# Second layer's tiles as 4, 4, 4, 4 and 1 instead of 4, 4, 4, 3 and 2, with quarter-sum products in the fourth block too

## The chip, the cores and the metric

The kernel runs on one core of one Trainium2 chip. The metric is the device time of one execution in microseconds (us); lower is better. Before the change the median of 3 runs is 708.11 us (707.74 to 708.77).

## What is computed

Cross attention between 512 tokens and 32 states for 4 batches of 8 heads, then two dense layers over the 4 x 544 = 2176 rows that come out of it (17 tiles of 128 rows), each with an activation between its two weight matrices:

```python
attn_out = _attn_ref(x, state)                 # (4, 8, 544, 64)
x = attn_out.transpose(0, 2, 1, 3).reshape(2176, 512)
h = x @ w_in                                   # 512 -> 2048
x = elu(h) @ w_out                             # 2048 -> 512, first layer
h = x @ w2_in                                  # 512 -> 2048, second layer
g = h * np.tanh(np.log1p(np.exp(np.minimum(h, 20.0))))
out = g @ w2_out                               # 2048 -> 512
```

The results are float32. The change is in the second layer alone.

## The kernel before, in words

**Products.** To multiply in float32 with TensorE's single-pass type float32r, an operand is split into a high half (rounded by a copy to float32r) and a low half (what is left). A product of two operands is then three instructions: high x high, high x low, low x high. They are lines 935 to 937 (first multiplication, `mm1`: 128 x 128 of `w_in` is loaded into the array, the rows of x stream through), 1138 to 1140 (second multiplication, `mm2`: 128 x 128 of the activation g is loaded, 512 columns of `w_out` stream) and 1066 to 1068 (the same with quarter sums). Where an operand is not split (line 911, the first layer's state tile; line 776, the attention's scores), a float32 product is issued as two instructions by the compiler.

**The second layer.** `BLOCKS2` (line 39) gives its blocks as (first tile, tiles): four tiles each in blocks 0, 1 and 2, three in block 3, two in block 4. A block goes through 16 steps, one for each slice j of 128 of the 2048 hidden units. A step is `mm1` (4 parts of the contraction x 3 instructions of 128 columns per tile), `hidden` (the activation on ScalarE and VectorE, lines 991 to 1002, and the split of g) and, two steps later, `mm2` (3 instructions of 512 columns for each tile of the block).

**Quarter sums.** Blocks in `SEVEN` (1 and 2) do the second multiplication by Strassen's scheme: for a pair of slices, a 2 x 2 arrangement of quarters of g and of w_out is multiplied with seven products instead of eight. `g_sums` makes the sums of g's quarters on VectorE; those of w_out (the factors) are made once, kept in device memory (`f2d`, `h2d`) and loaded again for each pair (`load_factors`). `seven_products` issues 7 x 6 instructions of 256 columns per pair, two of the seven behind the even step's `mm1` and five behind the odd step's. The seven results lie in seven of the eight PSUM banks, so each `mm1` shares the one that is left, and ScalarE copies it out at once (line 974). After a block's last pair the seven results are copied out and added up (`result_sums`, line 1087) during the next block's steps.

**The last two blocks** multiply plainly. Their steps go in groups of four (`GROUP`): four `mm1` in a row, then the four `mm2` held back. `halves_back` loads the split w_out again (16 x 512 KB) when block 2 ends. In block 4 the last results are copied in two halves by ScalarE and VectorE and stored by both queues (`retire`, lines 1173 to 1185).

**Order.** Every operation goes into `Plan` with a cost, its predecessors and a due time; `T` holds the due time of each step, summed from modelled costs (`mm(n)` = n / 2400 + 0.013 us). `Plan.run` then plays the operations and writes an order for each engine: the operation that can start first goes first, among equals the one that is due first. On the chip each engine follows its order. Buffers come from tags with a fixed number of places (`w_in` and `w_out`: 16 each; `o`: 4), and a load waits until a place is free. Loads and stores are issued by SP, in order.

Of the kernel before, what the change touches and what calls it, by code (L numbers as in the profile page):

```python
# [37 lines left out]
STATE_AT = NC  # L38
BLOCKS2 = [(0, 4), (4, 4), (8, 4), (12, 3), (15, 2)]

# [195 lines left out]
def attention_elu_mish(  # L236
# [95 lines left out]
    first2 = len(steps)  # L332
    steps += [(2, blk, t0, n, j) for blk, (t0, n) in enumerate(BLOCKS2) for j in range(NF)]
    index = {(k, b, j): s for s, (k, b, _, _, j) in enumerate(steps)}

    def mm1_cost(kind, blk, n, j):
        if kind == 0:
            return 16 * mm(4 * P)
        if kind == 1:
            return 2 * mm(4 * S) if (blk, j) in WHOLE else 6 * mm(S)  # L340
        return 12 * mm(n * P)

# [7 lines left out]
    for s, (kind, blk, t0, n, j) in enumerate(steps):  # L350
        c = mm1_cost(kind, blk, n, j) + (mm2_cost(kind, n, whole_out(kind, blk, j)) if kind < 2 else
                                         (30 if j % 2 else 12) * mm(HALF_E) if blk in SEVEN else n * 3 * mm(DM))
        T.append(T[-1] + c + (PACE_FIRST if s < NF // 2 else PACE if s < first2 else 0.0))
# [181 lines left out]
    def halves_back(j):  # L535
        w = w_sb["out", 2, j] = buf("w", "w_out", NF, [P, 2, DM], F32R, f"w_again{j}_")
        add(SP, 512.0, lambda: nc.sync.dma_start(out=w.t.bitcast(F32), in_=h2d[:, j]), r=[("h2d", j)],
            w=[(w, 0), (w, 1)], after=[products[max(products) - (j < NF // 2)][FREED[j % 8]]], lag=2.0)

# [357 lines left out]

    def apart(s):
        kind, blk, t0, n, j = steps[s]
        return kind == 2 and n < MAXC and j % GROUP < 2  # L900

    def mm1(s):
# [4 lines left out]
        if kind == 0:  # L907
            for i in range(NC):
                def f(i=i):
                    for k in range(NK):  # L910
                        nc.tensor.matmul(h[:, i * P:(i + 1) * P], lhsT=place_w1(j * NC + i, k),  # L911
                                         rhs=sread[:, k, :], start=(k == 0), stop=(k == NK - 1))

                sl = j * NC + i
                A("PE", 4 * mm(4 * P), f, w=[h], due=due,
                  r=[(w1[sl // 2], sl % 2)] + [("sread", b) for b in range(B)])
        elif kind == 1 and (blk, j) in WHOLE:
            for k in range(2):
                def f(k=k):
                    m = m_sb[blk, j // NC][:, k, j % NC * P:(j % NC + 1) * P]  # L920
                    nc.tensor.matmul(h.t, lhsT=m, rhs=x1[blk][:, k, :], start=(k == 0), stop=(k == 1))  # L921

                add("PE", mm(4 * S), f, w=[h], due=due,
                    r=[(m_sb[blk, j // NC], j % NC, q) for q in range(2)] + [(x1[blk], k)])
        else:
            nk = 2 if kind == 1 else NK
            for k in range(nk):
                def f(k=k):
                    if kind == 1:
                        wh, wl = (m_hl[s][:, i, k, :] for i in range(2))  # L930
                        xh, xl = (x1hl(blk)[:, i, k, :] for i in range(2))
                    else:
                        wh, wl = (w_sb["in", 2, j][:, i, k * P:(k + 1) * P] for i in range(2))
                        xh, xl = (x2[blk][i][:, k, :n] for i in range(2))
                    nc.tensor.matmul(h[:, :n], lhsT=wh, rhs=xh, start=(k == 0), stop=False)  # L935
                    nc.tensor.matmul(h[:, :n], lhsT=wh, rhs=xl, start=False, stop=False)  # L936
                    nc.tensor.matmul(h[:, :n], lhsT=wl, rhs=xh, start=False, stop=(k == nk - 1))  # L937

                if kind == 1:
                    r = [(m_hl[s], 0), (m_hl[s], 1), (x1hl(blk), k)]  # L940
                else:
                    w = w_sb["in", 2, j]
                    r = [(w, 0), (w, 1), (x2[blk][0], k), (x2[blk][1], k)]
                add("PE", 3 * mm(n), f, r=r, w=[h], due=due)
        return h

    def hidden(s, h):
# [4 lines left out]
        if kind < 2:  # L952
# [15 lines left out]
            split_g(g, e, 0, n, [e])  # L968
            return
        u = buf("l2", "u", 2, [P, MAXN])  # L970
        g = None
        if seven or kind == 2 and s - index[2, max(SEVEN), NF - 1] in COPIED:
            ps, h = h, buf("work", "wraw", 3, [P, MAXN], F32, "hs")
            add("ACT", act(n * P), lambda n=n: nc.scalar.copy(h[:, :n * P], ps[:, :n * P]), r=[ps], w=[h])
        if seven:
            pass
        elif apart(s):
            g = buf("l2", "g", 2, [P, 2, n * P], F32R, "g")
        else:
            g = buf("work", "g", GBUFS, [P, 2, MAXN], F32R, "g")  # L980
        gs[s] = g
        last = s == len(steps) - 1
        parts = [(0, n // 2), (n // 2, n)] if last else [(0, n)]
        if g:
# [23 lines left out]

    evens, g_factors = {}, {}

# [37 lines left out]
    def seven_products(s):  # L1048
# [8 lines left out]
        for o, k in enumerate(SEVEN_ORDER):  # L1057
# [4 lines left out]
            def run(a=acc[k], g=g[gi], gc=gc, f=f[fi], fc=fc):  # L1062
                for q in range(2):
# [6 lines left out]
            made[k] = add("PE", 6 * mm(HALF_E), run, r=gk + fk, w=[acc[k]],  # L1070
                          due=T[s + 1 + (o >= 2)] + SEVEN_DUE + 0.5 * o)
        if p < NF // 2 - 1:
            return
        due = T[s + 2] + 2.0
        o = {c: buf("work", "o", OBUFS, [P, DM], F32, f"o{blk}_{c}_") for c in ("11", "12", "21", "22")}
# [5 lines left out]
        for i, sums in enumerate(SUMS):  # L1081
            begin(s + SUMS_AT[i], result_sums, sums, v, t0)

    def result_sums(sums, v, t0):

        for to, a, b, op in sums:
            add("DVE", 0.605, lambda to=to, a=a, b=b, op=op: nc.vector.tensor_tensor(
                v[to].t, v[a].t, v[b].t, getattr(ALU, op)), r=[v[a], v[b]], w=[v[to]])
            if to in RESULTS:
                i, e = RESULTS[to]  # L1090
                for q in range(2):
                    add(SP, 128.0, lambda to=to, q=q, t=t0 + 2 * i + q, e=e: nc.sync.dma_start(
                        out=out_rows(t)[..., e * HALF_E:(e + 1) * HALF_E],
                        in_=v[to][:, q * HALF_E:(q + 1) * HALF_E]), r=[v[to]], due=T[len(steps)])

# [6 lines left out]
    def mm2(s, only=None):  # L1102
# [7 lines left out]
        if part not in accs:  # L1110
            tags = ["h"] if kind == 0 else [f"acc{i}" for i in range(NK if kind == 1 else n)]
            accs[part] = [spot(t, f"acc{kind}_{blk}_{t}_") for t in tags]
# [4 lines left out]
        due = T[s + 2]  # L1117
        made = []
        for i in (range(NC if kind < 2 else n) if only is None else only):
            acc = accs[part][0 if kind == 0 else i]  # L1120
# [28 lines left out]
    def retire(kind, blk, j, acc, s):  # L1149
        due = T[s + 2] + 4.5  # L1150

# [119 lines left out]
    for j in range(NF):  # L1271
        begin(index[1, 3, j], reload, "in", j)
        begin(min(index[1, 3, j] + 1, first2), reload, "out", j)
        begin(index[2, max(SEVEN), NF - 1] + 1 + j // 4, halves_back, j)
    for p in range(NF // 2):
        g = index[2, min(SEVEN) - 1, 0] + FACTORS_FROM + int(p * FACTORS_STEP)
        begin(g, make_factors, p, T[g + FACTORS_TO])
    for blk in sorted(SEVEN):
        for p in range(NF // 2):
            begin(index[2, blk, 0] + 2 * p if blk > min(SEVEN) or p > 1 else index[2, blk, 0] - 4 + 2 * p,  # L1280
                  load_factors, blk, p)
    for blk in range(len(BLOCKS2)):
        begin(first2 + NF * (blk - 1) + 6 if blk else s_state + NQ + 4, load_x2, blk)
    if WHOLE_J < NF:
# [4 lines left out]

    narrow = next(index[2, blk, 0] for blk, (_, n) in enumerate(BLOCKS2) if n < MAXC)  # L1290
    held = []
    for s in range(len(steps) + 2):
        if s < len(steps):
            kind, blk, t0, n, j = steps[s]
            if s == s_state + NQ + 3:

                switch.append(add("X", 0.0, flip, after=attention, due=T[first2] - 40.0))
            gate[:] = [*turn, *first] if s == narrow else turn if s > narrow else []
            h = mm1(s)
            turn = first = [plan.ops[-1]]  # L1300
            gate[:] = turn
            for f, args in later.pop(s, ()):
                f(*args)
            gate[:] = []
            hidden(s, h)
        if s < len(steps) and s >= narrow and (s - narrow) % GROUP < GROUP - 1 and \
                not (steps[s - 2][0] == 2 and steps[s - 2][1] in SEVEN):
            held.append(s - 2)
            continue
        if s == len(steps):  # L1310
            for i in range(BLOCKS2[-1][1]):
                for q in range(s - 2, s):
                    mm2(q, [i])
        elif s >= 2 and s < len(steps):
            gate[:] = turn if held else []
            turn = []
            for q in (*held, s - 2):
                turn = mm2(q)
                if held:
                    gate[:] = turn[-1:]  # L1320
                for j in after_step.pop(q, ()):
                    split_weight("out", 1, j, w_sb["whole", 1, j])
            held.clear()
            gate[:] = []
    assert not later
# [14 lines left out]
HALF_E = DM // 2  # L1340
SEVEN = {1, 2}
FIRST = [(0, 0, HALF), (1, 0, HALF), (0, HALF, NF), (1, HALF, NF), (2, 0, NF), (3, 0, NF)]
# [11 lines left out]
OBUFS = 4  # L1354
GROUP = 4
STATES_LATE = None
# [17 lines left out]
FREED = (1, 7, 4, 4, 6, 6, 3, 3)  # L1374
COPIED = (1,)
LATE_COPY = 0.0
# [32 lines left out]
```

## Time and profile before

| | |
|---|---|
| median of 3 runs | 708.11 us (707.74 to 708.77) |
| the profiled execution | 707.95 us |
| its span | 706.1 us |
| TensorE busy | 701.0 us, 99% |
| weight loads busy | 592.5 us, 84% |
| VectorE / ScalarE busy | 584.5 us (83%) / 452.9 us (64%) |

The span runs from the first to the last instruction; the execution has 1.85 us more around it. PE is TensorE's matmul, PEld its weight load (it overlaps PE), DVE VectorE, ACT ScalarE, SP the engine that issues most DMAs. Times in rows are us from the span's start unless marked ns. The time of one matmul in a row includes its way through the array; matmuls overlap, so their spacing is shorter. The chain of waits follows the work that ended last: each of its pieces begins where the one before it ends.

### The profile page before, as it was taken

The numbers are of one execution on the slowest core, as the hardware profiler recorded it, in microseconds if no ns is written. First come the engines' busy times: TensorE is split into PE (matmuls) and PEld (weight loads), VectorE is DVE, ScalarE is ACT, GpSimd is POOL, SyncE is SP. The second block draws the span as 40 slices with busy tenths as digits, with TensorE's granted clock in tenths as the row PEclk, the third lists the DMA queues.
The fourth block names the chain that finished last, engine by engine and source line by source line (L and its number), as shares of the span: only waits on it lengthen the run. The fifth ranks groups of instructions, "written<-read, shape, count | busy, mean of one in ns | idle before, by whom it ended". The sixth has DMA issues, their size and how long they took to land.

```text
span 706.1 us, 12109 instructions
## 1 busy us (share of the span) xinstructions
PE 701.0 (99%) x4370; PEld 592.5 (84%) x4370; DVE 584.5 (83%) x1176; ACT 452.9 (64%) x840; POOL 12.0 (2%) x26
## 2 busy tenths in 40 slices
PE   9999999999999999999999999999999999999998
PEld 7478787877888788888888888989989989999987
DVE  7999998969787867887889987798888998776575
ACT  4987775655666744675666657666776767554454
POOL 1000100100000000000000000000000000000000
PEclk9999999999999999999999999999999999999999
DMA  9846788374797877668778896665566459400100
GB/s 296 290 148 194 225 196 231 93 153 86 242 245 253 259 258 251 227 220 293 237 257 310 267 344 222 222 204 164 182 184 225 152 176 365 153 15 31 46 1 30
DMA packets 113826, 140.31 MB, mean 199 GB/s; under 512 B 48872, under 2 KB 77544, under 8 KB 113768
## 3 DMA queue, kind: packets, MB, share of 16 engines
q1 hardware_dynamic: 113352, 139.36, 61.9%
q8 instruction: 34, 0.56, 0.3%
q10 hardware_dynamic: 416, 0.20, 0.1%
q14 instruction: 24, 0.20, 0.1%
HBM read 101.25 MB, written 38.27 MB: 198 GB/s over the span
## 4 chain that ended last, share of the span: by engine, by line
PE 97%; DVE 1%; ACT 1%; DMA 1%; SPq 0%; issue 0%
PE acc_acc L1138 13%; PE h L935 13%; PE h L936 13%; PE h L937 13%; PE acc_acc L1140 13%; PE acc_acc L1139 13%; PE m L1068 4%; PE m L1067 4%; PE m L1066 4%; PE fold L614 2%; PE h L911 2%; PE h L921 1%; DMA st_raw<-in_state 1%; PE sr L859 1%; PE acc_acc L1126 1%; PE acc_h L1138 1%
## 5 line engine op out<-in xcount | busy, mean ns | idle before, releaser
L935 PE MATMUL h<-x,w_in 128*128 128x512 f32 (+2 forms) x320 | 114.6, 358 | 0.0
L936 PE MATMUL h<-x,w_in 128*128 128x512 f32 (+2 forms) x320 | 114.6, 358 | 0.0
L937 PE MATMUL h<-x,w_in 128*128 128x512 f32 (+2 forms) x320 | 114.2, 357 | 0.0
L1098 ACT CAST g<-e 128x512 fp32r<-128x512 f32 (+3 forms) x116 | 66.3, 572 | 68.1 <-PE acc_acc L1140 35.7
L1138 PE MATMUL acc_acc<-g,w_out 128*128 128x512 f32 x252 | 100.3, 398 | 0.0
L1139 PE MATMUL acc_acc<-g,w_out 128*128 128x512 f32 x252 | 98.2, 390 | 0.0
L1140 PE MATMUL acc_acc<-g,w_out 128*128 128x512 f32 x252 | 98.1, 389 | 0.0
L1099 DVE TENSOR_TENSOR g<-e,g 128x512 fp32r<-128x512 f32 (+3 forms) x116 | 72.9, 629 | 23.3 <-ACT g L1098 22.3
L996 ACT ACTIVATE e<-u,two 128x512 f32<-128x512 f32 (+3 forms) x81 | 53.0, 656 | 36.6 <-DVE u L994 36.5
L937 PEld LDWEIGHTS h<-x,w_in 128*128 128x128 f32 x320 | 60.3, 189 | 7.7
L935 PEld LDWEIGHTS h<-x,w_in 128*128 128x128 f32 x320 | 60.5, 189 | 7.0
L936 PEld LDWEIGHTS h<-x,w_in 128*128 128x128 f32 x320 | 60.5, 189 | 6.7
L1000 DVE TENSOR_TENSOR u<-u,e 128x512 f32<-128x512 f32 (+3 forms) x81 | 48.7, 603 | 19.7 <-ACT e L998 18.0
L1068 PE MATMUL m<-f,g 128*128 128x256 f32 x224 | 63.4, 283 | 0.0
L1067 PE MATMUL m<-f,g 128*128 128x256 f32 x224 | 63.4, 283 | 0.0
L1066 PE MATMUL m<-f,g 128*128 128x256 f32 x224 | 63.2, 282 | 0.0
L955 ACT ACTIVATE e<-h 128x512 f32<-128x512 f32 x68 | 40.3, 597 | 33.4 <-PE h L937 21.3
L1138 PEld LDWEIGHTS acc_acc<-g,w_out 128*128 128x128 f32 x252 | 47.4, 188 | 12.8 <-issue 1.7
L1140 PEld LDWEIGHTS acc_acc<-g,w_out 128*128 128x128 f32 x252 | 47.3, 188 | 10.0
L1139 PEld LDWEIGHTS acc_acc<-g,w_out 128*128 128x128 f32 x252 | 47.3, 188 | 9.8 <-issue 0.5
L992 DVE TENSOR_SCALAR e<-e 128x512 f32<-128x512 f32 (+3 forms) x81 | 30.8, 381 | 29.8 <-ACT e L991 29.5
L964 DVE SCALAR_TENSOR_TENSOR e<-e,h 128x512 f32<-128x512 f32 x67 | 45.5, 680 | 10.7 <-ACT e L957 10.6
(189 smaller groups left out, 1533.7 us busy)
## 6 DMA issues: line engine op xcount, KB each, us to landing
raw_in<-in_moe_w_in SPq DMA_DIRECT2D x32, 512.0 KB, 5.9
raw_out<-in_moe_w_out SPq DMA_DIRECT2D x32, 512.0 KB, 4.4
f<-f2d SPq DMA_DIRECT2D x32, 512.0 KB, 4.4
w2d<-wv SPq DMA_DIRECT2D x32, 256.0 KB, 3.3
f2d<-f SPq DMA_DIRECT2D x32, 256.0 KB, 3.5
h2d<-w_out SPq DMA_DIRECT2D x16, 512.0 KB, 6.2
f<-h2d SPq DMA_DIRECT2D x16, 512.0 KB, 4.8
w_again<-h2d SPq DMA_DIRECT2D x16, 512.0 KB, 8.4
```

Of the source, the lines that this page charges most:

```text
L935: nc.tensor.matmul(h[:, :n], lhsT=wh, rhs=xh, start=(k == 0), stop=False)
L936: nc.tensor.matmul(h[:, :n], lhsT=wh, rhs=xl, start=False, stop=False)
L937: nc.tensor.matmul(h[:, :n], lhsT=wl, rhs=xh, start=False, stop=(k == nk - 1))
L996: add("ACT", act(n) + 0.1, lambda c=c: nc.scalar.activation(e[:, c], u[:, c], AF.Ln, bias=two), r=[ku, "two"], w=[ke])
L1066: nc.tensor.matmul(out, lhsT=g[:, 0, c], rhs=f[:, 0, w], start=not p and not q, stop=False)
L1067: nc.tensor.matmul(out, lhsT=g[:, 0, c], rhs=f[:, 1, w], start=False, stop=False)
L1068: nc.tensor.matmul(out, lhsT=g[:, 1, c], rhs=f[:, 0, w], start=False, stop=p == NF // 2 - 1 and q == 1)
L1098: add("ACT", act(n), lambda: nc.scalar.copy(g[:, 0, c], e[:, c]), r=r, w=[(g, 0, q)])
L1099: add("DVE", dve(n), lambda: nc.vector.tensor_tensor(g[:, 1, c], e[:, c], g[:, 0, c].bitcast(F32), ALU.subtract), r=[*r, (g, 0, q)], w=[(g ...
L1138: nc.tensor.matmul(acc.t, lhsT=st[:, 0, :], rhs=mv[:, 0, :], start=fst, stop=False)
L1139: nc.tensor.matmul(acc.t, lhsT=st[:, 0, :], rhs=mv[:, 1, :], start=False, stop=False)
L1140: nc.tensor.matmul(acc.t, lhsT=st[:, 1, :], rhs=mv[:, 0, :], start=False, stop=lst)
```

## The change

The fourth block gets four tiles and goes with quarter sums (`SEVEN = {1, 2, 3}`); one tile is left, the odd one. Its `mm1` and activation come in four extra steps that stand behind the slices j = 5, 9, 11 and 13 of the fourth block; each does four slices of the odd tile side by side in one bank (48 instructions of 128 columns), and one activation of 512 columns. Its `mm2` (16 x 3 instructions of 512 columns) is put behind all other steps. The grouping in fours (`GROUP`, `held`, `apart`) goes away. `halves_back` loads the split w_out for the odd tile alone, 12 of 16 slices into places of the tag `w_in`, which come free as the odd tile uses up its slices. The fourth block's result sums are due at the end, since no block follows.

```diff
-BLOCKS2 = [(0, 4), (4, 4), (8, 4), (12, 3), (15, 2)]
+BLOCKS2 = [(0, 4), (4, 4), (8, 4), (12, 4), (16, 1)]
...
+    extra = len(BLOCKS2) - 1
+    for blk, (t0, n) in enumerate(BLOCKS2[:extra]):
+        for j in range(NF):
+            steps.append((2, blk, t0, n, j))
+            if blk == extra - 1 and j in EXTRA_BEHIND:
+                steps.append((2, extra, *BLOCKS2[extra], EXTRA_BEHIND.index(j)))
...
-        return 12 * mm(n * P)
+        return 12 * mm(n * P) if n > 1 else 48 * mm(P)
...
     def halves_back(j):
-        w = w_sb["out", 2, j] = buf("w", "w_out", NF, [P, 2, DM], F32R, f"w_again{j}_")
+        w = w_sb["out", 2, j] = buf("w", "w_in" if j < 12 else "w_out", NF, [P, 2, DM], F32R, f"w_again{j}_")
...
-            w=[(w, 0), (w, 1)], after=[products[max(products) - (j < NF // 2)][FREED[j % 8]]], lag=2.0)
+            w=[(w, 0), (w, 1)], after=list(products[max(products)].values()) if j >= 12 else (), lag=2.0)
...
+        elif kind == 2 and n == P:
+            for i in range(4):
+                w = w_sb["in", 2, 4 * j + i]
+
+                def f(i=i, w=w):
+                    o = h[:, i * P:(i + 1) * P]
+                    for k in range(NK):
+                        wh, wl = (w[:, q, k * P:(k + 1) * P] for q in range(2))
+                        xh, xl = (x2[blk][q][:, k, :P] for q in range(2))
+                        nc.tensor.matmul(o, lhsT=wh, rhs=xh, start=(k == 0), stop=False)
+                        nc.tensor.matmul(o, lhsT=wh, rhs=xl, start=False, stop=False)
+                        nc.tensor.matmul(o, lhsT=wl, rhs=xh, start=False, stop=(k == NK - 1))
+
+                add("PE", 12 * mm(P), f, w=[h], due=T[s - 1] + EXTRA_DUE + 0.01 * i,
+                    r=[(w, 0), (w, 1)] + [(x2[blk][q], k) for q in range(2) for k in range(NK)])
...
-        if seven or kind == 2 and s - index[2, max(SEVEN), NF - 1] in COPIED:
+        if seven or kind == 2 and blk == extra:
...
+        if kind == 2 and blk == extra:
+            for i in range(4):
+                r = 4 * j + i
+                w = w_sb["out", 2, r]
+
+                def f(i=i, w=w, r=r, a=accs[part][0]):
+                    st = g[:, :, i * P:(i + 1) * P]
+                    nc.tensor.matmul(a.t, lhsT=st[:, 0, :], rhs=w[:, 0, :], start=not r, stop=False)
+                    nc.tensor.matmul(a.t, lhsT=st[:, 0, :], rhs=w[:, 1, :], start=False, stop=False)
+                    nc.tensor.matmul(a.t, lhsT=st[:, 1, :], rhs=w[:, 0, :], start=False, stop=r == NF - 1)
+
+                add("PE", 3 * mm(DM), f, r=[(g, p, 0) for p in range(2)] + [(w, 0), (w, 1)], w=[accs[part][0]],
+                    due=T[len(steps)] + EXTRA_TO + 0.7 * r, after=last_copy)
...
-        begin(index[2, max(SEVEN), NF - 1] + 1 + j // 4, halves_back, j)
+        begin(index[2, extra, j // 3 if j < 9 else 3] + 1 + (j >= 12), halves_back, j)
...
+    for j in range(NF // 4):
+        mm2(index[2, extra, j])
...
-SEVEN = {1, 2}
+SEVEN = {1, 2, 3}
...
+EXTRA_BEHIND = (5, 9, 11, 13)
+EXTRA_DUE, EXTRA_TO, LAST_TO = 1.75, 10.0, 6.0
```

## Rows read from the trace of the kernel before

**Rows 1.** The page: busy us per engine; granted clock in 40 slices.

```profile
PE 701.0 (99%) x4370; PEld 592.5 (84%) x4370; DVE 584.5 (83%) x1176; ACT 452.9 (64%) x840; POOL 12.0 (2%) x26
...
PEclk9999999999999999999999999999999999999999
```

**Rows 2.** Busy us by stretch: block 2, block 3, block 4, tail.

```profile
core 0: us, PE busy (x) PEld busy (x) DVE busy (x) ACT busy (x) POOL busy (x), PEclk, DMA share, GB/s
501.83:585.99 84.16, 84.16 (x531) 76.29 (x529) 75.28 (x154) 58.84 (x113) 0.00 (x0) 1.00 0.59 190
585.99:653.11 67.12, 67.12 (x363) 62.04 (x362) 50.80 (x106) 37.41 (x76) 0.00 (x0) 1.00 0.35 131
653.11:702.64 49.53, 49.47 (x307) 44.08 (x305) 31.17 (x87) 26.65 (x71) 0.00 (x0) 1.00 0.05 17
702.64:706.10 3.46, 0.00 (x0) 0.00 (x0) 0.42 (x1) 0.37 (x1) 0.00 (x0) 1.00 0.45 152
```

**Rows 3.** Instructions by shape, whole span: count, busy us, mean ns, idle before.

```profile
L1140 PE MATMUL acc_acc<-w_again,g 128*128 128x512 f32 x80 | 31.2, 390 | 0.0
...
L937 PE MATMUL h<-x,w_in 128*128 128x384 f32 x64 | 21.4, 335 | 0.0
...
L937 PE MATMUL h<-x,w_in 128*128 128x256 f32 x64 | 18.1, 283 | 0.0
...
L911 PE MATMUL h<-sread,w 128*128 128x128 f32 x128 | 15.2, 275 | 0.0
```

**Rows 4.** Chain of waits (start us, us, what), end of block 2.

```profile
575.63 0.23 PE h L935
...
578.38 0.11 PE m L1066
...
579.81 0.23 PE h L935
...
582.56 0.12 PE m L1066
...
586.15 0.18 PE h L935
```

**Rows 5.** Chain of waits: 48 products of three tiles, first, and what follows.

```profile
636.72 0.17 PE h L935
...
645.06 0.23 PE acc_acc L1138
```

**Rows 6.** Chain of waits: 48 products of two tiles, first, and what follows.

```profile
653.26 0.12 PE h L935
...
659.02 0.23 PE acc_acc L1138
```

**Rows 7.** Chain of waits: last 36 second-multiplication products, first and last.

```profile
694.44 0.23 PE acc_acc L1138
...
702.40 0.24 PE acc_acc L1140
```

**Rows 8.** Short products: line 776's loads in the timeline; line 911 in the chain.

```profile
6.57 0.97 PEld L776 LDWEIGHTS scores<-sd,xT 128*128 128x128 f32 x8 [0.39 <-issue]
...
259.99 2.01 PE h L911 x18
```

**Rows 9.** Weight loads by shape, whole span: count, busy us, mean ns.

```profile
L937 PEld LDWEIGHTS h<-x,w_in 128*128 128x128 f32 x320 | 60.3, 189 | 7.7
...
L776 PEld LDWEIGHTS scores<-sd,xT 128*128 128x128 f32 x64 | 7.6, 191 | 1.1 <-issue 1.1
...
L859 PEld LDWEIGHTS sr<-xb,raw 128*32 128x32 f32 x128 | 2.1, 110 | 0.0
```

**Rows 10.** Timeline of ScalarE: the copy behind a first multiplication in block 2.

```profile
578.42 0.59 ACT L974 COPY hs<-h 128x512 f32<-128x512 f32 x1 [1.37 <-PE h L937]
```

**Rows 11.** Activation steps on VectorE by shape, in block 2.

```profile
L1000 DVE TENSOR_TENSOR u<-u,e 128x512 f32<-128x512 f32 x16 | 11.0, 690 | 3.7 <-ACT e L998 3.0
...
L992 DVE TENSOR_SCALAR e<-e 128x512 f32<-128x512 f32 x16 | 6.7, 420 | 1.3 <-ACT e L991 1.3
```

More of the change, by code (lines that the diff above doesn't have):

```diff
@@ L332, in attention_elu_mish @@
     first2 = len(steps)
-    steps += [(2, blk, t0, n, j) for blk, (t0, n) in enumerate(BLOCKS2) for j in range(NF)]
+    extra = len(BLOCKS2) - 1
[4 more added lines that the diff above has]
+                steps.append((2, extra, *BLOCKS2[extra], EXTRA_BEHIND.index(j)))
+    plain = [s for s, st in enumerate(steps) if st[:2] != (2, extra)] + [len(steps), len(steps) + 1]
     index = {(k, b, j): s for s, (k, b, _, _, j) in enumerate(steps)}
@@ L351, in attention_elu_mish @@
         c = mm1_cost(kind, blk, n, j) + (mm2_cost(kind, n, whole_out(kind, blk, j)) if kind < 2 else
-                                         (30 if j % 2 else 12) * mm(HALF_E) if blk in SEVEN else n * 3 * mm(DM))
+                                         (30 if j % 2 else 12) * mm(HALF_E) if blk in SEVEN else n * 3 * mm(DM) if n > 1 else 0.0)
         T.append(T[-1] + c + (PACE_FIRST if s < NF // 2 else PACE if s < first2 else 0.0))
@@ L896, in split_first @@
                 r=[(v, hf), (t, hf, 0)], w=[(t, hf)])
-    def apart(s):
-        kind, blk, t0, n, j = steps[s]
-        return kind == 2 and n < MAXC and j % GROUP < 2
     def mm1(s):
@@ L969, in hidden @@
             return
+        if n == 1:
+            n = 4
         u = buf("l2", "u", 2, [P, MAXN])
         g = None
-        if seven or kind == 2 and s - index[2, max(SEVEN), NF - 1] in COPIED:
+        if seven or kind == 2 and blk == extra:
             ps, h = h, buf("work", "wraw", 3, [P, MAXN], F32, "hs")
-            add("ACT", act(n * P), lambda n=n: nc.scalar.copy(h[:, :n * P], ps[:, :n * P]), r=[ps], w=[h])
+            last_copy[:] = [add("ACT", act(n * P), lambda: nc.scalar.copy(h.t, ps.t), r=[ps], w=[h])]
         if seven:
             pass
-        elif apart(s):
-            g = buf("l2", "g", 2, [P, 2, n * P], F32R, "g")
+        elif blk == extra and kind == 2:
+            g = buf("w", "w_in", NF, [P, 2, MAXN], F32R, "g")
         else:
@@ L981, in hidden @@
         gs[s] = g
-        last = s == len(steps) - 1
-        parts = [(0, n // 2), (n // 2, n)] if last else [(0, n)]
+        parts = [(0, n)]
         if g:
@@ L1007, in hidden @@
                 split_g(g, e, c0 * P, c1 * P, [ke], q)
-    evens, g_factors = {}, {}
+    evens, g_factors, last_copy = {}, {}, []
     def g_sums(s, e, ke):
@@ L1070, in seven_products @@
             made[k] = add("PE", 6 * mm(HALF_E), run, r=gk + fk, w=[acc[k]],
-                          due=T[s + 1 + (o >= 2)] + SEVEN_DUE + 0.5 * o)
+                          due=T[plain[min(plain.index(s) + 1 + (o >= 2), len(plain) - 1)]] + (SEVEN_DUE if s < plain[-3] else LAST_TO) + 0.5 * o)
         if p < NF // 2 - 1:
             return
-        due = T[s + 2] + 2.0
+        due = T[s + 2] + 2.0 if blk < max(SEVEN) else T[len(steps)] + LAST_TO + 8.0
         o = {c: buf("work", "o", OBUFS, [P, DM], F32, f"o{blk}_{c}_") for c in ("11", "12", "21", "22")}
@@ L1081, in seven_products @@
         for i, sums in enumerate(SUMS):
-            begin(s + SUMS_AT[i], result_sums, sums, v, t0)
+            if blk < max(SEVEN):
+                begin(s + SUMS_AT[i], result_sums, sums, v, t0)
+            else:
+                result_sums(sums, v, t0)
     def result_sums(sums, v, t0):
@@ L1093, in result_sums @@
                         out=out_rows(t)[..., e * HALF_E:(e + 1) * HALF_E],
-                        in_=v[to][:, q * HALF_E:(q + 1) * HALF_E]), r=[v[to]], due=T[len(steps)])
+                        in_=v[to][:, q * HALF_E:(q + 1) * HALF_E]), r=[v[to]], due=T[len(steps)] + 20.0)
     def split_g(g, e, c0, c1, r, q=0):
@@ L1110, in mm2 @@
         if part not in accs:
-            tags = ["h"] if kind == 0 else [f"acc{i}" for i in range(NK if kind == 1 else n)]
+            tags = ["h"] if kind == 0 or kind == 2 and blk == extra else [f"acc{i}" for i in range(NK if kind == 1 else n)]
             accs[part] = [spot(t, f"acc{kind}_{blk}_{t}_") for t in tags]
@@ L1118, in mm2 @@
         made = []
+        if kind == 2 and blk == extra:
[9 more added lines that the diff above has]
+                    due=T[len(steps)] + EXTRA_TO + 0.7 * r, after=last_copy)
+            if j == NF // 4 - 1:
+                retire(kind, blk, j, accs.pop(part), s)
+            return made
         for i in (range(NC if kind < 2 else n) if only is None else only):
@@ L1149, in retire @@
     def retire(kind, blk, j, acc, s):
-        due = T[s + 2] + 4.5
+        due = T[s + 2] + 4.5 if kind < 2 or blk != extra else T[len(steps)] + EXTRA_TO + 14.0
         def place(name):
@@ L1279, in attention_elu_mish @@
         for p in range(NF // 2):
-            begin(index[2, blk, 0] + 2 * p if blk > min(SEVEN) or p > 1 else index[2, blk, 0] - 4 + 2 * p,
+            begin(index[2, blk, 2 * p] if blk > min(SEVEN) or p > 1 else index[2, blk, 0] - 4 + 2 * p,
                   load_factors, blk, p)
     for blk in range(len(BLOCKS2)):
-        begin(first2 + NF * (blk - 1) + 6 if blk else s_state + NQ + 4, load_x2, blk)
+        begin(index[2, min(blk, extra - 1) - 1, 6 + 4 * (blk == extra)] if blk else s_state + NQ + 4, load_x2, blk)
     if WHOLE_J < NF:
@@ L1288, in attention_elu_mish @@
             begin(max(0, s - 3), fold_slice, s)
-    narrow = next(index[2, blk, 0] for blk, (_, n) in enumerate(BLOCKS2) if n < MAXC)
-    held = []
     for s in range(len(steps) + 2):
@@ L1297, in attention_elu_mish @@
                 switch.append(add("X", 0.0, flip, after=attention, due=T[first2] - 40.0))
-            gate[:] = [*turn, *first] if s == narrow else turn if s > narrow else []
             h = mm1(s)
-            turn = first = [plan.ops[-1]]
-            gate[:] = turn
+            gate[:] = [plan.ops[-1]]
             for f, args in later.pop(s, ()):
@@ L1305, in attention_elu_mish @@
             hidden(s, h)
[L1306 to L1324, printed above, removed]
+        if s >= 2 and (steps[s - 2][0] != 2 or steps[s - 2][1] != extra):
+            mm2(s - 2)
+            for j in after_step.pop(s - 2, ()):
+                split_weight("out", 1, j, w_sb["whole", 1, j])
+    for j in range(NF // 4):
+        mm2(index[2, extra, j])
     assert not later
@@ L1354 @@
 OBUFS = 4
-GROUP = 4
 STATES_LATE = None
@@ L1374 @@
 FREED = (1, 7, 4, 4, 6, 6, 3, 3)
-COPIED = (1,)
+EXTRA_BEHIND = (5, 9, 11, 13)
+EXTRA_DUE, EXTRA_TO, LAST_TO = 1.75, 10.0, 6.0
 LATE_COPY = 0.0
```

## The prediction

> **What bounds the kernel now.** I read the page's busy line and clock line first: TensorE is busy 99% of the span, and its granted clock is full in every slice, 1.00 of 2.4 GHz [rows 1, 2]. Then the stages of the second layer's end, in the view that cuts the span into stretches [rows 2]: block 2 (a block with quarter sums) from 501.83 to 585.99 us, the three-tile block to 653.11, the two-tile block to 702.64, and 3.46 us of tail in which TensorE does nothing. In the first three stretches TensorE is busy in all but 0.06 us. VectorE reaches 75.3 of 84.2 us in block 2 and less behind it; transfers hold a DMA share of 0.59, 0.35 and 0.05. So the end is set by how fast TensorE takes its instructions, and the change has to be summed as TensorE instructions times their spacing.
>
> A row's mean duration is not that spacing: it holds the way through the array as well (335 ns for 384 columns, 283 ns for 256 [rows 3]). The spacing is read in the chain of waits, where each piece begins where the one before it ends. Twelve 512-column products of a first multiplication beside quarter sums take 575.63 to 578.38 = 2.75 us; the 42 products of 256 columns of a pair take 1.43 + 3.59 = 5.02 us [rows 4]. 48 products of 384 columns take 636.72 to 645.06 = 8.34 us, 0.1738 each [rows 5]. 48 of 256 columns take 653.26 to 659.02 = 5.76 us, 0.1200 each [rows 6]. 36 of the second multiplication (512 columns) take 694.44 to 702.64 = 8.20 us, 0.2278 each [rows 7].
>
> **Part 1, TensorE's work.** I sum from 586.15 us, where block 2's last first multiplication is done and the one before the change starts its three-tile block; the last 42 quarter-sum products of block 2 (5.02 us) follow in both.
> Before: 5.02 + 192 x 0.1738 (three tiles, 16 slices of 12) = 33.36, + 192 x 0.1200 (two tiles) = 23.04, + 240 second-multiplication products (80 on each of three lines [rows 3]) x 0.2278 = 54.67. Sum 116.09 us. The trace has 702.64 - 586.15 = 116.49, so 0.40 us are small waits.
> After, with p for one 128-column product of the odd tile: 5.02 + 16 x 2.75 = 44.00, + 8 pairs x 5.02 = 40.16, + 48 second-multiplication products of one tile x 0.2278 = 10.93, + 192 p. Sum 100.11 + 192 p.
> The two are equal at p = 0.0853 us. The whole sign hangs on one number that no row has: the trace holds no product of this kind (three-term, single-pass) narrower than 256 columns.
>
> **Part 2, the price of a 128-column product.** Every product has its own weight load of 128 x 128; consecutive ones with the same weights load them again (lines 935 to 937 have equal counts of loads and products). Two kinds of row bound p.
> From below, by columns: 0.2278, 0.1738 and 0.1200 for 512, 384 and 256 columns fall by 0.054 for every 128, so 128 columns would take 0.066, if columns still set the spacing.
> By the load: the eight products of line 776 stream only 64 columns, but their loads start (0.97 - 0.19) / 7 = 0.111 us apart; line 911 streams 128 columns and 18 of them take 2.01 us, 0.1117 each [rows 8]. Halving the columns changed nothing, so there the 128 x 128 load sets the pace. Both are full-precision products, but the load is the same: 189 ns in the single-pass product, 191 in the full one; a load of only 32 columns takes 110 [rows 9]. The difference, 80 ns for 96 columns, makes 0.107 us of port time for 128 columns, which a narrower moving side can't shorten.
> I take p = 0.1117 (line 911 has the same shape); ends 0.107 (the port alone) and 0.120 (no gain at all over 256 columns, if the 0.012 us that doesn't go with the columns, 0.1200 - 2 x 0.054, comes on top). The odd tile's first multiplication then costs 21.45 us, almost as much as the two-tile block's 23.04: halving the columns buys 1.6 us.
> After = 121.56, against 116.49: **+5.07 us**. The same in other terms: quarter sums save 192 x 0.2278 - 336 x 0.1195 = 3.58 us in the block, and the move of a tile from one block to the other costs the rest, because 192 x (0.2278 + 0.1117) is more than 192 x (0.1738 + 0.1200), by 8.77 us; the 0.40 of small waits go, and 192 products cost 0.0014 more beside quarter sums.
>
> A rule of the Trainium skill speaks for another p: "TensorE: Matmul & The Clock Gate", section "Back-to-back issue gap", gives a sustained 81 ns per product at 128 columns in a stream of load and product pairs. By that the sum is 100.11 + 15.55 = 115.66 and the change gains 0.8 us. The same list has 131 ns for 512 columns, where the trace has 228 [rows 7], so I give it little.
>
> **Part 3, what lies beside.** VectorE and ScalarE: a pair of slices in block 3 has the load of one in block 2, and an odd-tile step adds one more chain of 512 columns: on VectorE 0.42 + 4 x 0.69 = 3.2 us [rows 11] beside 5.4 us of TensorE. Block 3 then asks (75.3 + 12.7) of some 106 us, 83%, less than block 2's 89% [rows 2]. Cost 0; if p were 0.066 it would still be 88 of 97.
> PSUM: quarter sums hold seven of eight banks, so each first multiplication needs the one bank that ScalarE has just copied out. After a first multiplication 1.43 us of products cover that copy, which starts at once and takes 0.59 [rows 10]. The odd tile's work is due behind two products (1.43 us), and three more follow it (2.15). Cost 0; without the cover at most 0.8 us at each of eight hand-overs.
> Transfers: 16 reloads of 512 KB of w_out move from the start of the three-tile block into block 3, twelve of them into w_in's places as the odd tile frees them. That is 8 MB more in some 106 us that otherwise load as block 2 did (0.59 share); on SP the last four wait for pair 6's products, with the result stores behind them, and are needed some 13 us later. Cost 0.
> The end: after block 3's last first multiplication its chain is some 14 dependent steps of at most 0.69 (estimate: under 9.7 us). TensorE has 30 + 12 products of older pairs and the odd tile's 48: 3.59 + 1.43 + 10.93 = 15.95 us. The last 42 products fit into this, and their copies and seven sums lie beside the rest of the odd tile's products. What then is late is the odd tile's copy and store, as the last tile's now: I keep 3.46 us [rows 2].
>
> **The sum.** 586.15 + 121.56 + 3.46 = 711.17 us of span; the profiled execution has 707.95 - 706.1 = 1.85 us around it: 713.02. It ran 0.16 below the median of the runs, 708.11, so the forecast is **713.2 us**; p at its ends makes that 712.3 to 714.8.
>
> **The rivals.**
> A, the forecast: the load sets the spacing. For it: two lines with different widths at one spacing. Against: neither is single-pass. Chance 0.65.
> B, block 3's closing comes out last: its seven copies, seven sums and eight stores no longer lie under a following block. Price up to 7 x 0.69 = 4.8 us, if all of VectorE's sums stand behind the last product; half of it gives 715.6, all of it 718.0. It decides once the last 42 products end less than about 5 us ahead of the odd tile's last. Against: 16 us of cover for under 10. Chance 0.13.
> C, columns set the spacing after all: loads of a single-pass product overlap each other more than line 776's do. Then p = 0.066, 192 p = 12.7, and the time is 713.2 - 8.7 = 704.4: faster. It decides from p below 0.0853. For it: three widths on one straight line. Against: line 776. Chance 0.07.
> D, loads overlap in part, so that p lies midway between C's and A's, 0.089: 100.11 + 17.1 = 117.2 us, +0.7, 708.8, no change by what this kernel's measurement can tell (0.2%, 1.4 us). For it: the single-pass load is 2 ns shorter than line 776's [rows 9]; against: a spacing of 0.111 wherever columns don't decide. Chance 0.06. The rate of the Trainium skill's page named above would be of this kind.
> E, a narrow single-pass product is run as a full-precision one. Line 911's 64 products appear as 128 instructions [rows 3], two spacings each: p = 2 x 0.1117 = 0.223, +21.4 us, 734.6. For it: the trace has no narrow single-pass row at all. Against: 256 columns sit exactly on the single-pass line. Chance 0.09.
>
> **How the numbers follow.** 713.2 is A's. From 706 to 718.5 the range holds D, A with its bounds and B to its full price, 0.84 less a little at the edges; C and E stay out. Faster by over 0.2%: C and a little of D, 0.08. Within 0.2%: the rest of D and A's lowest edge, 0.07. Slower: 0.85.
>
> **What will show it.** The spacing of the odd tile's first multiplication in the chain of waits: 0.11 to 0.12 for A, 0.066 for C, 0.22 for E. Its 48 products of one step should take 5.4 us, with loads end to end and TensorE's busy line still at 99%. The quarter-sum products of block 3 should keep 1.43 and 3.59 us, and no wait of TensorE above 0.2 us should stand at the odd steps. After TensorE's last instruction some 3.5 us should be left, with the odd tile's copy in them; sums there instead would be B. The prediction is wrong in its core if p is below 0.0853, and in its size if the tail or the hand-overs take more than 2 us.

## The result, and the profile after

The changed kernel takes 713.62 us (median of 4 runs, 713.24 to 713.98) beside 707.92 us for the kernel before: ratio 1.0079, 95% interval 1.0062 to 1.0096. It is slower by 5.7 us; the forecast was 713.2, 5.1 above the median it was made against.

The page of the changed kernel: busy us per engine, the granted clock in 40 slices.

```profile
PE 705.6 (99%) x4514; PEld 597.2 (84%) x4514; DVE 602.2 (85%) x1180; ACT 461.8 (65%) x827; POOL 11.6 (2%) x26
...
PEclk9999999999999999999999999999999999999999
```

TensorE is still what ends last, at full clock as before [rows 1]; it has 4.6 us more of busy time.

Busy us by stretch after the change: block 2, block 3 with the odd steps, the end of TensorE's work, the tail. The cut at 690.90 lies 2.2 us behind block 3's last first multiplication, which ends at 688.66 in the chain.

```profile
core 0: us, PE busy (x) PEld busy (x) DVE busy (x) ACT busy (x) POOL busy (x), PEclk, DMA share, GB/s
501.83:586.13 84.30, 84.30 (x530) 76.43 (x529) 76.11 (x159) 58.10 (x110) 0.00 (x0) 1.00 0.61 197
586.13:690.90 104.77, 104.77 (x717) 96.94 (x716) 85.33 (x170) 69.58 (x129) 0.00 (x0) 1.00 0.56 197
690.90:707.54 16.64, 16.62 (x96) 14.33 (x94) 12.88 (x23) 4.46 (x8) 0.00 (x0) 1.00 0.52 198
707.54:711.20 3.66, 0.00 (x0) 0.00 (x0) 0.42 (x1) 0.37 (x1) 0.00 (x0) 1.00 0.31 102
```

These answer to [rows 2]. Block 2 ends where it ended. Behind it TensorE stands still nowhere, and its last instruction ends at 707.54 instead of 702.64 us. The tail is 3.66 us instead of 3.46.

The chain of waits at the second odd step (start us, us, what): the last quarter-sum product before it, the first and last of its 48 products, the product that follows.

```profile
641.62 0.12 PE m L1086
641.74 0.06 PE h L936
641.80 0.12 PE h L937
641.91 0.11 PE h L938
642.02 0.11 PE h L936
...
646.82 0.11 PE h L937
646.94 0.11 PE h L938
647.05 0.17 PE m L1084
```

This is the row that was missing before: a three-term product of 128 columns. From 641.74 to 647.05 the 48 take 5.31 us, 0.1106 each, like the full-precision line 911 [rows 8] and not the 0.066 of the line through [rows 5 to 7].

### The profile page after: what moved, and what is told of

Same layout as the page of the kernel before. It is cut to its first block, busy times and chain, and to the rows that moved or that the text cites. A ratio compares the mean times of both kernels' runs of the same rounds, so it can differ in the third digit from the quotient of the medians.

```text
span 711.2 us, 12456 instructions
## 1 busy us (share of the span) xinstructions
PE 705.6 (99%) x4514; PEld 597.2 (84%) x4514; DVE 602.2 (85%) x1180; ACT 461.8 (65%) x827; POOL 11.6 (2%) x26
## 4 chain that ended last, share of the span: by engine, by line
PE 97%; DMA 2%; SPq 0%; ACT 0%; issue 0%; DVE 0%; ACTq 0%
PE h L952 12%; PE h L953 12%; PE h L954 12%; PE acc_acc L1175 10%; PE acc_acc L1176 10%; PE acc_acc L1177 10%; PE m L1086 6%; PE m L1084 6%; PE m L1085 6%; PE fold L620 2%; PE h L913 2%; PE h L923 1%; DMA raw_in<-in_moe_w_in 1%; PE h L937 1%; PE h L938 1%; PE h L936 1%
## 5 line engine op out<-in xcount | busy, mean ns | idle before, releaser
L952 PE MATMUL h<-x,w_in 128*128 128x512 f32 x256 | 100.2, 391 | 0.0
L953 PE MATMUL h<-x,w_in 128*128 128x512 f32 x256 | 100.2, 391 | 0.0
L954 PE MATMUL h<-x,w_in 128*128 128x512 f32 x256 | 99.6, 389 | 0.0
L1086 PE MATMUL m<-f,g 128*128 128x256 f32 x336 | 95.1, 283 | 0.0
L1085 PE MATMUL m<-f,g 128*128 128x256 f32 x336 | 95.1, 283 | 0.0
L1119 ACT CAST g<-e 128x512 fp32r<-128x512 f32 x87 | 54.1, 621 | 63.1 <-PE acc_acc L1177 34.9
L1084 PE MATMUL m<-f,g 128*128 128x256 f32 x336 | 95.0, 283 | 0.0
L1120 DVE TENSOR_TENSOR g<-e,g 128x512 fp32r<-128x512 f32 x87 | 60.0, 690 | 19.1 <-ACT g L1119 18.1
L1014 ACT ACTIVATE e<-u,two 128x512 f32<-128x512 f32 x68 | 49.3, 725 | 32.3 <-DVE u L1012 32.2
L1018 DVE TENSOR_TENSOR u<-u,e 128x512 f32<-128x512 f32 x68 | 46.8, 689 | 26.3 <-ACT e L1016 24.7
L1085 PEld LDWEIGHTS m<-f,g 128*128 128x128 f32 x336 | 64.3, 191 | 1.9
L1084 PEld LDWEIGHTS m<-f,g 128*128 128x128 f32 x336 | 64.3, 191 | 1.9
L1086 PEld LDWEIGHTS m<-f,g 128*128 128x128 f32 x336 | 64.3, 191 | 0.0
L954 PEld LDWEIGHTS h<-x,w_in 128*128 128x128 f32 x256 | 48.1, 188 | 10.4
L952 PEld LDWEIGHTS h<-x,w_in 128*128 128x128 f32 x256 | 48.2, 188 | 8.8
```

The source lines that it names most:

```text
L1014: add("ACT", act(n) + 0.1, lambda c=c: nc.scalar.activation(e[:, c], u[:, c], AF.Ln, bias=two), r=[ku, "two"], w=[ke])
L1084: nc.tensor.matmul(out, lhsT=g[:, 0, c], rhs=f[:, 0, w], start=not p and not q, stop=False)
L1085: nc.tensor.matmul(out, lhsT=g[:, 0, c], rhs=f[:, 1, w], start=False, stop=False)
L1086: nc.tensor.matmul(out, lhsT=g[:, 1, c], rhs=f[:, 0, w], start=False, stop=p == NF // 2 - 1 and q == 1)
L1119: add("ACT", act(n), lambda: nc.scalar.copy(g[:, 0, c], e[:, c]), r=r, w=[(g, 0, q)])
L1120: add("DVE", dve(n), lambda: nc.vector.tensor_tensor(g[:, 1, c], e[:, c], g[:, 0, c].bitcast(F32), ALU.subtract), r=[*r, (g, 0, q)], w=[(g ...
```

## The experiments

**What sets 0.111 us.** A narrower load, a narrower and a wider stream tell the load from the columns and from a fixed price per instruction. (The changed kernel's 713.62 us and the runs below were measured at different times. The median of the kernel before stayed between 707.84 and 708.11 us meanwhile, so a difference between them is good to some 0.3 us.)

```diff
-                        nc.tensor.matmul(o, lhsT=wh, rhs=xl, start=False, stop=False)
-                        nc.tensor.matmul(o, lhsT=wl, rhs=xh, start=False, stop=(k == NK - 1))
+                        nc.tensor.matmul(o[:P // 2], lhsT=wh[:, :P // 2], rhs=xl, start=False, stop=False)
+                        nc.tensor.matmul(o[:P // 2], lhsT=wl[:, :P // 2], rhs=xh, start=False, stop=False)
```

(The full product stands first in the first part and last in the others.) 

> The changed kernel, but the two low-half products of each part of the odd tile's first multiplication load only 64 of the 128 weight columns (half of the low-half terms is left out); the moving side stays 128 columns. Weight load sets the spacing (my theory): 64 full loads keep 0.111 us, 128 half loads need about 0.057 and so fall to the columns' 0.066; 64 x (0.333 - 0.243) = 5.8 us less, 707.8 us. Rival, a floor of 0.111 us under every short product whatever it loads: 713.6, no change. Rival, columns alone: 713.6 too, since they stay.

Measured: 707.06 us (median of 10 runs, nine of them from 706.41 to 707.67 and one at 712.88; ratio to the kernel before 0.9991, 0.9975 to 1.0007), 6.6 less than the changed kernel. That is 0.8 more than expected, since a half load goes with 0.060 us and not with 0.066: 64 x (0.333 - 0.111 - 2 x 0.060) = 6.5. The chain of waits of this kernel:

```profile
615.97 0.06 PE h L938
616.03 0.06 PE h L939
616.09 0.11 PE h L941
616.20 0.06 PE h L938
616.26 0.06 PE h L939
616.32 0.11 PE h L941
```

Lines 938 and 939 load 64 columns, line 941 loads 128, and all three stream 128. The spacing goes with the load, 0.06 to 0.11. It even falls below 0.066 (a step's 48 products take 3.71 us; 16 full loads of 0.111 are 1.78 of it, and the rest is 0.060 each), so the 0.012 us that the forecast's straight line carried at 256 to 512 columns isn't paid in full here. A floor of 0.111 us under every product is refuted.

The stream halved instead:

```diff
+                        nc.tensor.matmul(o[:, :P // 2], lhsT=wh, rhs=xl[:, :P // 2], start=False, stop=False)
+                        nc.tensor.matmul(o[:, :P // 2], lhsT=wl, rhs=xh[:, :P // 2], start=False, stop=(k == NK - 1))
```

> The changed kernel, but the two low-half products of each part stream only 64 of 128 columns (half of the low-half terms is left out); loads stay 128 wide. Load theory: spacing stays 0.111 us, 713.6 us. If the columns had a share in the spacing: up to 128 x 0.027 = 3.4 us less, 710.2.

Measured: 719.73 us, ratio 1.0165 (1.0151 to 1.0179): 6.1 us *slower* than the changed kernel, which neither side had expected. The chain of waits shows why.

```profile
644.92 0.14 PE h L936
645.06 0.08 PE h L937
645.14 0.11 PE h L938
645.25 0.14 PE h L936
645.40 0.10 PE h L937
645.50 0.21 PE h L938
645.72 0.27 PE h L936
645.98 0.16 PE h L937
```

Up to 645.4 three products take 0.33 us as in the changed kernel; from there they take 0.64. The same stretches by busy time and granted clock, and two more around the third odd step:

```profile
638.00:645.50 7.50, 7.50 (x57) 7.05 (x56) 5.90 (x13) 4.61 (x11) 0.00 (x0) 0.99 0.43 120
645.50:652.30 6.80, 6.80 (x33) 6.80 (x34) 3.82 (x8) 2.84 (x6) 0.00 (x0) 0.51 1.02 387
...
661.00:668.00 7.00, 7.00 (x55) 7.00 (x55) 4.21 (x9) 2.65 (x6) 0.00 (x0) 0.84 0.40 105
668.00:675.00 7.00, 7.00 (x31) 6.22 (x31) 3.32 (x7) 3.50 (x7) 0.00 (x0) 0.67 1.01 377
```

The granted clock is 0.99 in the first and 0.51 in the second, half of 2.4 GHz (1.2 GHz), although TensorE is busy in both from end to end. It fell a second time between 661 and 675 us. The clock that is missing in these rows adds up to 0.49 x 6.80 + 0.16 x 7 + 0.33 x 7 = 6.8 us, enough for the 6.1. In the first and the fourth odd step, with the same products, the clock stayed at 1.00 and the 48 products took 5.30 and 5.28 us, 0.110 each: at full clock the spacing is what the load theory says. To test whether the clock is all of the loss, one of the two products got its 128 columns back:

```diff
+                        nc.tensor.matmul(o, lhsT=wh, rhs=xl, start=False, stop=False)
+                        nc.tensor.matmul(o[:, :P // 2], lhsT=wl, rhs=xh[:, :P // 2], start=False, stop=(k == NK - 1))
```

> As half_cols, but only the last of the three products of each part streams 64 columns; the second has its 128 again (half of the low-weight terms is left out). If half_cols was slower only because the granted clock fell (0.62 in 645 to 654 us) and the clock stays at 1.00 here: spacing 0.111 us and 713.6 us. If narrow products cost time of their own: three more us than the changed kernel, half of what half_cols lost, 716.7. If the clock falls here too, the trace shows it in the granted clock and the time lies between.

Measured: 713.25 us (ratio 1.0076, 1.0061 to 1.0091). The stretch with the second odd step:

```profile
641.00:648.00 7.00, 7.00 (x64) 7.00 (x63) 4.71 (x9) 4.24 (x9) 0.00 (x0) 1.00 0.88 279
```

The granted clock is 1.00, and an odd step takes 5.28 or 5.29 us (5.31 in the changed kernel). So narrow products cost nothing of their own and save next to nothing; the 6.1 us were the clock.

The stream doubled:

```diff
-                    o = h[:, i * P:(i + 1) * P]
+                    o = h[:, i // 2 * 2 * P:(i // 2 + 1) * 2 * P].rearrange("p (t f) -> p t f", t=2)
...
+                        xh, xl = (v.unsqueeze(1).to_broadcast([P, 2, P]) for v in (xh, xl))
```

> The changed kernel, but each product of the odd tile's first multiplication streams its 128 columns twice, 256 in all (its results are added up twice and not meant to be used). Load theory: the spacing goes from 0.111 only to the 256-column 0.120 us, 192 x 0.009 = 1.7 us more, 715.3. If columns had a share: up to 192 x 0.054 = 10.4 us more, 724.0.

Measured: 715.16 us (ratio 1.0100, 1.0084 to 1.0115), 1.5 us more, with a spacing of 0.12 in the chain:

```profile
620.39 0.12 PE h L937
620.51 0.12 PE h L938
620.63 0.12 PE h L939
620.75 0.12 PE h L937
```

Twice the columns for 0.009 us a product: the 128 columns that the new cut of the tiles leaves out had been almost free.

**The two parts of the change.** The new cut alone, without quarter sums in the fourth block:

```diff
-SEVEN = {1, 2, 3}
+SEVEN = {1, 2}
```

(with `halves_back` as in the kernel before.) 

> One part alone: tiles as 4, 4, 4, 4, 1, but the fourth block multiplies plainly, without quarter sums (192 products of 512 columns for 336 of 256; split w_out is loaded at block 2's end as before). By the sum: 192 x 0.2278 = 43.7 us instead of 40.2, and 192 first products 0.0014 cheaper: 3.3 us more than the changed kernel, 716.9, and 9 us more than the kernel before: the new cut of the tiles alone is what costs. Rival, quarter sums in the fourth block cost more than their products (sums, copies, shared bank): 713.6 or less.

Measured: 718.60 us (ratio 1.0156, 1.0141 to 1.0171), 1.7 more than the sum. TensorE's timeline, with the idle time before an instruction and what ended it in brackets, names most of the extra:

```profile
592.07 0.39 PE L1084 MATMUL m<-f,g 128*128 128x256 f32 x1 [0.48 <-ACT g L1043]
...
593.19 0.39 PE L1086 MATMUL m<-f,g 128*128 128x256 f32 x1 [0.62 <-DVE g L1045]
```

These two waits are 1.1 us. Block 2's last products run without a first multiplication between them: the fourth block's first step, now plain, keeps the one free bank until its activation is done (VectorE reads the bank last from 595.21 to 595.89, and the next first multiplication begins at 595.95). The kernel before copies it out there (`COPIED`), and the changed code has no such line. With it:

```diff
-        if seven or kind == 2 and blk == extra:
+        if seven or kind == 2 and (blk == extra or s == index[2, max(SEVEN), NF - 1] + 1):
```

> As plain4 (4, 4, 4, 4, 1 without quarter sums in the fourth block), with one line put right: the first step behind the last quarter-sum block copies its first product out of PSUM at once, as the kernel before does; in plain4 TensorE waited 1.5 us there for the one free bank. Expected: 718.6 - 1.6 = 717.0, which is the sum's 716.9, so quarter sums in the fourth block are worth 3.3 us. Rival: the loss moves on, 718.6.

Measured: 716.78 us (ratio 1.0128, 1.0111 to 1.0145). That is the sum's 716.9, and TensorE's two waits are gone. So the new cut of the tiles costs 8.7 us over the kernel before measured beside it (708.09), and quarter sums give 3.2 of them back against the changed kernel's 713.62.

**The cover at the end.**

```diff
-EXTRA_DUE, EXTRA_TO, LAST_TO = 1.75, 10.0, 6.0
+EXTRA_DUE, EXTRA_TO, LAST_TO = 1.75, 0.0, 30.0
```

> The changed kernel with the order at the end turned round: the odd tile's 48 second-multiplication products are due before the fourth block's last 42 quarter-sum products, so that the fourth block's copies, sums and stores come out last. If the odd tile's products are a needed cover: between one sum and all seven sums of VectorE behind the last product, 1.3 to 4.8 us more, 715 to 718.4. Rival, TensorE has no other cover for the last activation either way and the closing is short: 713.6 to 714.5.

Measured: 716.14 us (ratio 1.0127, 1.0110 to 1.0144), 2.5 more than the changed kernel. The end of its chain of waits:

```profile
705.26 0.13 PE m L1086
...
705.42 0.59 ACT o L296
...
707.19 1.86 DMA out<-o
...
709.17 0.70 DVE o L296
709.90 0.69 DVE o L1108
```

TensorE is done at 707.5 as in the changed kernel, but the last copy of the fourth block waits for a place of the tag `o` that a store has to empty (`DMA out<-o`), and the last sum (line 1108) ends 3 us behind TensorE. In the changed kernel the last quarter-sum product ends at 700.70, the same line is done at 705.35, and both lie beside the odd tile's last 30 products:

```profile
704.67 0.68 DVE L1108 TENSOR_TENSOR o<-u_wv,o 128x512 f32<-128x512 f32 x1
707.97 0.42 DVE L296 COPY o<-acc_h 128x256 f32<-128x256 f32 x1 [2.61 <-ACT o L296]
```

**A version that needs fewer loads.** If the load is the price, the odd tile should be multiplied in the way that loads least. A full-precision product is two instructions, two loads; three terms are three. The odd tile's x and weights stay unsplit.

```diff
+                        nc.tensor.matmul(o, lhsT=w[:, i, k * P:(k + 1) * P], rhs=x2[blk][:, k, :P],
+                                         start=(k == 0), stop=(k == NK - 1))
...
+        w = w_full[i] = buf("l2", "x2", 1, [P, NK, MAXN], F32, f"w_full{i}_")
+        add(SP, 1024.0, lambda: nc.sync.dma_start(out=w.t, in_=w2d[:, 0, 4 * i:4 * i + 4, :]),
```

(The weights go into the place that x of the second layer was loaded through, which is free by then.) 

> The changed kernel, but the odd tile's first multiplication is done in full float32: unsplit weights are loaded from device memory (four slices, 1 MB, ahead of each odd step), and each of the 64 products is two instructions with a load each instead of three. Load theory: 64 x 2 x 0.1117 = 14.3 us instead of 21.3, so 7.0 less: 706.6, below the kernel before by 1.3. Rival, the shorter odd steps (3.6 us) no longer cover the vector work or the 1 MB loads and TensorE waits: 708 to 711. Rival, full float32 costs four passes over the columns, 0.226 us a product and 14.5 in all, which is the same number here and not told apart.

Measured: 706.32 us (7 runs, 705.77 to 707.21) beside 708.11 us for the kernel before, ratio 0.9972 (0.9962 to 0.9983). Its chain of waits has one odd step in one line:

```profile
616.31 0.12 PE m L1080
616.43 3.59 PE h L932 x32
620.02 0.12 PE m L1078
```

32 instructions in 3.59 us, 0.112 each, where the changed kernel has 48 in 5.31. The vector work and the loads still fit; TensorE has no wait behind block 2. This version beats both kernels, the one before by 1.8 us.

That its price is the load and not the columns can't be read from this run. A full-precision instruction of 512 columns takes 0.43 us in the kernel before:

```profile
29.91 0.86 PE h L921 x2
```

By that, 128 columns take 0.11 us, as much as their load. The row that tells the two apart is line 776: 64 columns, still 0.111 [rows 8].

## Why the prediction was right

**The price of a 128-column product** was taken as 0.1117 us, from a full-precision line and by the load. The chain of waits has 0.1106, so 192 of them are 21.2 us instead of the 21.45 of the sum. That the load sets it was argued from rows of other precision; the halved load and the halved and doubled streams show it. Of the two rows of the argument only line 776 carried it: line 911, whose price was taken over, would have 0.11 us by its columns alone (0.43 us for 512), so that its number fits is in part luck. The Trainium skill has the time of a load in "TensorE: Matmul & The Clock Gate", section "LDWEIGHTS (loading the stationary operand)": the number of columns divided by 1.2, in ns. By that a load of 128 columns takes 107 ns (an estimate from the page's formula); the trace agrees within 4 ns, with 0.111 us between starts. The 81 ns per pair that the same page's section "Back-to-back issue gap" gives for 128 columns isn't met here: the measurement decides, 0.111.

**The sum of TensorE's work** ended at 707.71; the trace has 707.54. Block 3 began 0.23 us earlier than in the kernel before (585.92 instead of 586.15 in the chain), and from there the work takes 121.62 us where the sum had 121.56. The quarter-sum products of block 3 keep their price: 12 of them take 1.43 or 1.44 us, 30 take 3.59 or 3.60, and the 18 behind an odd step 2.21 instead of 2.15, since the first of them takes 0.17.

**The work beside it** stayed hidden: VectorE has 85.33 of 104.77 us there, 81% where the sum had 83%. No wait of TensorE shows in the stretches. The reload of w_out cost nothing. The cover at the end was counted too high: where the prediction has 30 + 12 products of older pairs behind block 3's last first multiplication, the chain has 24, 2.88 us. With products of the odd tile and 12 of the last 42 between, there were still 8.4 us before the last 30 began, and TensorE waited for nothing.

**The tail** was kept at 3.46 and is 3.66 us, and the time outside the span of the profiled execution is 2.04 us (713.24 - 711.2) instead of 1.85. The profiled execution so takes 713.24 where the sum had 713.02; the rest of the way to 713.62 is that this time it ran 0.38 below the median, not 0.16. These differences are small and have nothing to do with the mechanism; the forecast of the change, 5.1 us, is 0.6 under the measured 5.7.

**The rivals.** The closing coming out last (B) is a real mechanism of the price that was named, 2.5 us when it is made to happen; the order of the changed kernel avoids it by 2.2 us (705.35 against 707.54). Columns alone (C), loads overlapping in part (D) and a full-precision fallback (E) are refuted by one row, the 0.1106.

## What to carry to other kernels

Before an odd tile is split off, price its products by the longer of two times, that of streaming the moving columns and that of loading the weights; below the width where they cross (here just under 256 columns, which take 0.120 us where the load takes 0.111), fewer columns buy next to nothing, and the number of loads is the cost. Where no row shows the new shape, look for a row with the same load and a narrower stream: if its spacing doesn't follow its columns, that spacing is the price. And where the load rules, choose the way of multiplying that loads least, even if it streams more: here full precision streams two times 0.11 us a product instead of three times 0.054, and is faster.

## What the runs showed of the hardware that was not expected

TensorE's granted clock can fall to half while its busy line reads 100%. With two of three products in an odd step cut to 64 columns, the clock went from 0.99 to 0.51 at 645.5 us and cost 6.1 us in all; with one of three cut it stayed at 1.00. What ran before the fall were 128-column loads at full rate with short streams between them. It fell around the second and the third of the four odd steps and not in the first and the fourth, which have the same products; what decides this the runs don't say. All four runs of this kernel have a mean clock of 0.99. In the full-precision version, whose 32 instructions a step have the same spacing, the granted clock is 1.00 around all four odd steps.

The 0.012 us that a three-term product takes beyond its columns at 256 to 512 columns doesn't appear in full at 128 columns with a 64-column load (0.060 us, of which 0.054 are 128 columns by the slope of [rows 5 to 7], leave 0.006). The runs don't say what it is.
